# Attention kernel on one core: first queries in two loads, second key group and first values requested together, two more shared chunks, first output batch in two pieces

## The chip, the cores and the metric

The kernel runs on one core of a Trainium2 chip. The metric is the device time of one execution in microseconds (us). The kernel before took 522.69 us in the median of five runs (521.66 to 522.73). One more execution was recorded by the hardware profiler; it took 522.24 us, and its profile is the one read here.

## The reference: what is computed

Grouped-query attention with a softmax over 512 keys and no mask:

```python
B, Hq, Hkv, Sq, Sk, D = 16, 32, 8, 288, 512, 128      # bf16
k, v = repeat(k, 4, axis=1), repeat(v, 4, axis=1)
p = softmax(einsum("bhqd,bhkd->bhqk", q, k) * D ** -0.5)
out = einsum("bhqk,bhkd->bhqd", p, v)
```

Four query heads share one key/value head. So there are 16 x 8 = 128 groups, each with 4 x 288 = 1152 query rows, 512 keys and 512 value rows.

## The kernel before

**Tiling.** A group's 1152 query rows are nine tiles of 128 (t = 0 to 8), its 512 keys four tiles of 128 (j = 0 to 3). The scores are made transposed, keys on the partitions, so each pair (t, j) is a block of 128 columns: 36 blocks for a group. They are packed into three chunks of 1536 columns, which is three PSUM banks of 512 (`CH`, `BANK`, `TPC = 3`). Function `place` (L356) says where: chunk 0 holds t 0-3 with j 0, 1 and 2, one bank each; chunk 1 holds t 0-3 with j 3, then t 4-7 with j 0 and 1; chunk 2 holds t 4-7 with j 2 and 3, then t 8 with all four j. Over the 128 groups the chunks are numbered n = 0 to 383.

**One chunk.** TensorE makes the scores S(n) in one of two PSUM halves of `ps_s` (`op_s`, L420; the matmuls are on L439). ScalarE takes the exponential of the chunk from PSUM to `pt_sb` in bf16 (`op_exp`, L498; L516, or L511 for all but the last piece where a chunk is cut). TensorE multiplies the exponentials by the values: batch PV(r), r = 0 to 383, makes the three output tiles t = 3b to 3b + 2 (b = r mod 3) with twelve matmuls of 129 columns (`op_pv`, L462; L479); the 129th column is the sum of the row, since `v_sb` holds a column of ones. VectorE takes the reciprocal of the sums (`op_rc`, L573, L575) and multiplies (`op_ev`, L578, L585) into `o_sb`, which SyncE stores (`op_store`, L332).

**Shared chunks.** In every sixth chunk from n = 6 (`shared`, L519) the last 120 columns are kept from ScalarE. TensorE makes their scores by a matmul of its own in a corner of `ps_o` (`op_sy`, L445, L450; it waits until the output batch n - 3 has been evicted), and VectorE makes their exponential with a polynomial: `op_y`, `op_yb`, two in `op_ym`, `op_yu` three times, `op_yp` (L527 to L556), eight instructions spread over two rounds of its loop. There are 63 such chunks, n = 6 to 378.

**The order is written out by engine.** TensorE: warm-up matmuls; transposes of group 0's keys (`op_kt`, L399, L404); then for each n S(n), the shared piece if there is one, and PV(n - 2). At n = 2 the keys of group 1 are transposed between S(2) and PV(0) (L663, L664). VectorE first copies the transposed keys of groups 0 and 1 to `kt_sb` (`op_kc`, L408, L411): group 0 in two copies (key tile 0, then 1 to 3), group 1 in one. Then it goes through r: reciprocal, shared work, eviction. GpSimd copies the values of each group from `vd_sb` to `v_sb` (`op_vc`, L561, L568). PV of a group waits for that copy. S(n) waits for its queries (`have_q`), its keys (`have`) and for the exponential of chunk n - 2, which frees its PSUM half.

**The first chunks.** Chunks n < `FIRST` = 2 are cut into three exponentials of one bank each, as is the last one, 383. For these the matmuls of a bank signal it alone (`s_s0`), the exponentials signal each (`s_eb`), and consumers wait for the bank they need (`ready`, L374).

**The first loads.** SyncE's queue takes, in this order (L626, L627): the queries of group 0 as one transposing DMA of nine tiles (`op_q0`, L313, L316), the values of group 0 (128 KB, `op_v`, L302), the queries of group 1 (L311), the keys of groups 2 and 3 (transposing, L291), the values of groups 1 to 3 (384 KB), the queries of groups 2 and 3. ScalarE's queue takes the keys of group 0 (128 KB, not transposed, L676 and L283), then runs a small exponential, waits until VectorE has made both copies of group 0's keys (`s_k0` at 2, L678), issues the load of group 1's keys (128 KB, L680), and only then begins the exponentials. All later loads and stores are on SyncE's queue, ordered by due times in chunks (L630 to L642).

Of the kernel before, what the change touches and what calls it, by code (L numbers as in the profile page):

```python
# [131 lines left out]
def bass_standalone__gqa_softmax__near_ridge_kernel(  # L132
# [37 lines left out]
    NQ = 12  # L170
    NPT = 6
    WARM = 5
    FIRST = 2
    FIRST_SHARED = 6
    AHEAD = 1.08
    NO = 12
    NS = NG * NC
    LASTG = NG - 1
    ALONE = 8 * TPC


# [6 lines left out]
    with ExitStack() as es:  # L188
# [123 lines left out]

        def op_q0(i):  # L313

            c0, c1 = 0, NT
            nc.sync.dma_start_transpose(qt_sb[:, 0, c0:c1], q_v[0:P, c0 * D:c1 * D]).then_inc(sem["s_qp%d" % i], 16)  # L316

        def have_q(g, i):
            if g == 0:
                return ("s_qp0", 16)  # L320
            return ("s_q%d" % (g % NQ), 16 * (g // NQ + (0 if g % NQ == 0 else 1)))

        def have(kind, g):
# [46 lines left out]
        def used(i):  # L370

            return max(b for b in range(NC) for t in range(b * TPC, (b + 1) * TPC) for j in range(NJ) if place(t, j)[0] == i)

        def ready(n, x):  # L374

            if n < FIRST and x < TPC - 1:
                return ("s_eb", n * (TPC - 1) + x + 1)
            return ("s_e", n + 1 + (x if n == NS - 1 else 0))

        def sequence(b):  # L380

# [38 lines left out]
        def op_s(n):  # L420
            eng = nc.tensor
            g, i = n // NC, n % NC
            sl, gi = (g // UG) % NSLOT, g % UG
            waits = [have("k", g), have_q(g, i)]
            if n >= 2 + FIRST:
                waits.append(("s_e", n - 1))
            qg = qt_sb[:, g % NQ].rearrange("d t p -> d (t p)")
            todo = pieces(i)
            for x, (c, j, t, w) in enumerate(todo):
                if shared(n) and c + w == CH:  # L430
                    w -= W
                w_x = waits if x == 0 else []
                if n == 0 and x < 2:
                    w_x = [("s_k0", 1), waits[1]] if x == 0 else waits[:1]
                if n == 1 and x < 2:
                    w_x = [have_q(g, x)]
                if 2 <= n < 2 + FIRST:
                    w_x = w_x + [ready(n - 2, c // BANK)]
                ins = emit(eng, w_x, lambda: eng.matmul(  # L439
                    ps_s[:, n % 2, c:c + w], kt_sb[:, sl, j, gi, :], qg[:, t * P:t * P + w], start=True, stop=True))  # L440
                if n < FIRST and (c + w) % BANK == 0 and c + w < CH:
                    ins.then_inc(sem["s_s0"], 1)
            ins.then_inc(sem["s_s"], 1)

# [14 lines left out]
                return ps_s[:, 0, 0:TPC * DV].rearrange("p (a e) -> p a e", e=DV)  # L459
            return ps_o[:, r % 2, 0:TPC * DV].rearrange("p (a e) -> p a e", e=DV)  # L460

        def op_pv(r):  # L462
            eng = nc.tensor
            g = r // NC
            sl, gi = (g // UG) % NSLOT, g % UG
            waits = [("s_vc", g + 1)]
            if 2 <= r < NS - 2:
                waits.append(("s_ev", r - 1))
            if r == NS - 2:
                waits.append(("s_e", NS - 1))  # L470


            todo = sequence(r % NC)
            for x, (t, j) in enumerate(todo):
                i, c = place(t, j)
                w_x = (waits if x == 0 else []) + [ready(g * NC + i, c // BANK)]
                if c == CH - P and shared(g * NC + i):
                    w_x.append(("s_yp", nth(g * NC + i)))
                ins = emit(eng, w_x, lambda: eng.matmul(  # L479
                    outs(r)[:, t - r % NC * TPC, :], pt(g, t, j), v_sb[:, sl, gi * NJ + j, 0:DV], start=(x == 0),  # L480
                    stop=(t not in [y[0] for y in todo[x + 1:]]), skip_group_check=True))
            ins.then_inc(sem["s_pv"], 1)

        def op_pv_last():

# [12 lines left out]
        def op_exp(n):  # L498
# [6 lines left out]
            parts = [(0, CH)]  # L505
            if shared(n):
                parts = [(0, CH - W)]
            if n < FIRST or n == NS - 1:
                parts = [(x, x + BANK) for x in range(0, CH, BANK)]
            for x, (c, e) in enumerate(parts[:-1]):  # L510
                ins = emit(eng, [("s_s0", (TPC - 1) * n + x + 1)] if n < FIRST else waits, lambda: eng.activation(  # L511
                    d[:, c:e], s[:, c:e], ACTF.Exp, scale=scale))
                ins.then_inc(sem["s_e" if n == NS - 1 else "s_eb"], 1)
            parts = [(d[:, c:e], s[:, c:e]) for (c, e) in parts[-1:]]
# [2 lines left out]


        def shared(n):  # L519
            return FIRST_SHARED <= n < NS - NC and (n - FIRST_SHARED) % EVERY == 0  # L520

        def nth(n):
            return (n - FIRST_SHARED) // EVERY + 1

        def op_y(n):
            eng, b = nc.vector, nth(n) % NB
# [96 lines left out]
                op0=ALU.is_lt, op1=ALU.add)).then_inc(sem["s_bad"], 1)  # L623


        first = [lambda: op_q0(0), lambda: op_v(0, None, 0, 1)]  # L626
        first += [lambda: op_q(1), lambda: op_k(0, 2), lambda: op_v(0, None, 1, UG), lambda: op_q(2), lambda: op_q(3)]  # L627

        sp = []
# [23 lines left out]
        def _(eng):  # L653
# [5 lines left out]
            for n in range(NS):  # L659
# [2 lines left out]
                    op_sy(n)  # L662
                if n == 2:  # L663
                    op_kt(1, range(NJ), 1)  # L664
                if n >= LAG:
                    op_pv(n - LAG)
            op_pv(NS - 2)
            op_pv_last()
# [6 lines left out]
        def _(eng):  # L675
            op_kd(eng, 0)  # L676
            eng.activation(dum[:], nc.const_aps.tensor(0.0, [P, 1], FP32), ACTF.Exp)
            for (s, n) in need(eng, [("s_k0", 2)]):  # L678
                eng.wait_ge(s, n)
            op_kd(eng, 1)  # L680
            for n in range(NS):
                op_exp(n)
# [84 lines left out]
```

## Time and profile before

| What | Value |
|---|---|
| median of five runs | 522.69 us (521.66 to 522.73) |
| profiled execution | 522.24 us |
| its span, first to last instruction | 520.5 us |
| TensorE matmuls, busy | 509.7 us (98%), 6118 recorded |
| ScalarE, busy | 513.4 us (99%) |
| VectorE, busy | 369.1 us (71%) |
| GpSimd, busy | 79.6 us (15%) |
| granted TensorE clock | 1.00 |
| first exponential starts | 4.91 us |
| last exponential of the first three chunks ends | 9.30 us |
| next exponential (chunk 3) starts | 9.84 us |
| last exponential (chunk 383, third piece) starts | 516.37 us |

All positions are microseconds from the start of the span. An engine's busy time counts its instructions from start to end; matmuls and exponentials overlap their neighbours, so a busy engine need not be the one that sets the pace. A row of the timeline joins neighbouring instructions of the same kind: start, length from the first start to the last end, engine, line, what is written and read, how many; in brackets the idle time of that engine before it and what ended it. PE is TensorE's matmuls, PEld its weight loads, DVE VectorE, ACT ScalarE, POOL GpSimd, SP SyncE; a q behind the name means the DMA-issuing queue of that engine.

### The profile page before, as it was taken

The page shows a single profiled execution, that of the slowest core. Times are in us where ns is not written, and L with a number is a line of the kernel's source. Part 1 is how long each engine was busy: PE and PEld are TensorE (multiplying, and loading weights), DVE is VectorE, ACT ScalarE, POOL GpSimd, SP SyncE. Part 2 cuts the span into 40 slices and gives each one's busy share as a digit, 9 for nine tenths or more (in the row PEclk, how much of TensorE's full clock was granted, in tenths as well). Part 3 has the DMA queues.
Part 4 walks back from the last instruction along what each step waited for, and adds up shares of the span by engine and source line. Part 5 has one row for each costly group of instructions (what it writes and reads, how often), then busy time and mean ns, then how long its engine had stood idle before and what let it go on. Part 6 is the DMA issues. An engine that isn't in the chain of part 4 may idle for free.

```text
span 520.5 us, 15243 instructions
## 1 busy us (share of the span) xinstructions
PE 509.7 (98%) x6118; PEld 394.4 (76%) x6224; DVE 369.1 (71%) x1315; ACT 513.4 (99%) x393; POOL 79.6 (15%) x135
## 2 busy tenths in 40 slices
PE   8999999999999999999999999999999999999997
PEld 4777777777777777777777777777777777777776
DVE  2767777677677677676776776767767767677776
ACT  6999999999999999999999999999999999999997
POOL 2111111111111111111111111111111111111110
PEclk9999999999999999999999999999999999999999
DMA  9999999999999999999999999999999999998212
GB/s 183 239 212 255 247 190 228 241 210 220 193 259 252 196 259 202 234 225 210 248 247 210 215 229 226 237 185 199 251 215 237 219 194 217 196 241 185 90 69 93
DMA packets 253078, 110.06 MB, mean 211 GB/s; under 512 B 219728, under 2 KB 236752, under 8 KB 253008
## 3 DMA queue, kind: packets, MB, share of 16 engines
q1 hardware_dynamic: 252720, 108.82, 99.4%
q8 instruction: 49, 0.80, 0.7%
q10 hardware_dynamic: 288, 0.26, 0.2%
q14 instruction: 21, 0.17, 0.1%
HBM read 17.04 MB, written 37.75 MB: 105 GB/s over the span
## 4 chain that ended last, share of the span: by engine, by line
ACT 97%; PE 1%; DMA 1%; issue 1%; DVE 0%
ACT pt_sb L516 97%; DMA kd_sb<-in_k_dram 1%; PE ps_o L417 0%; ACT pt_sb L511 0%; PE ps_o L404 0%; PE ps_s L439 0%; PE ps_o L479 0%; DVE o_sb L585 0%; DVE o_sb L595 0%; PE ps_s L479 0%; DVE kt_sb L411 0%; DVE rl_sb L575 0%; PE ps_o L669 0%; DVE bad_sb L621 0%; DVE flag_i L734 0%
## 5 line engine op out<-in xcount | busy, mean ns | idle before, releaser
L516 ACT ACTIVATE pt_sb<-ps_s 128x1536 bf16<-128x1536 f32 (+2 forms) x384 | 509.0, 1441 | 0.5 <-PE ps_s L439 0.5
L479 PE MATMUL ps_o<-v_sb,pt_sb 128*128 128x129 bf16 x4584 | 322.1, 220 | 1.1
L479 PEld LDWEIGHTS ps_o<-v_sb,pt_sb 128*128 128x128 bf16 x4584 | 282.7, 98 | 49.6 <-DVE o_sb L585 13.8
L439 PE MATMUL ps_s<-qt_sb,kt_sb 128*128 128x512 bf16 (+2 forms) x1430 | 290.0, 320 | 5.1 <-DMA qt_sb<-in_q_dram 0.5
L585 DVE TENSOR_TENSOR o_sb<-ps_o,rl_sb 128x384 bf16<-128x384 f32 x382 | 211.7, 554 | 9.3 <-DVE rl_sb L575 0.5
L439 PEld LDWEIGHTS ps_s<-qt_sb,kt_sb 128*128 128x128 bf16 x1536 | 123.7, 98 | 62.1 <-DMA qt_sb<-in_q_dram 0.7
L575 DVE RECIPROCAL rl_sb<-ps_o 128x3 f32<-128x3 f32 x382 | 67.7, 177 | 125.8 <-PE ps_o L479 124.3
L568 POOL COPY v_sb<-vd_sb 128x512 bf16<-128x512 bf16 x128 | 78.6, 615 | 429.8 <-PE ps_o L479 412.9
L549 DVE SCALAR_TENSOR_TENSOR u_sb<-u_sb,m_sb 128x120 f32<-128x120 f32 x126 | 35.6, 282 | 2.2
L556 DVE SCALAR_TENSOR_TENSOR pt_sb<-u_sb,e_sb 128x120 bf16<-128x120 f32 x63 | 17.8, 283 | 2.2
L549 DVE SCALAR_TENSOR_TENSOR u_sb<-m_sb 128x120 f32<-128x120 f32 x63 | 17.4, 276 | 0.0
L527 DVE TENSOR_SCALAR y_sb<-ps_o 128x120 f32<-128x120 f32 x63 | 15.9, 252 | 0.0
L540 DVE TENSOR_SCALAR m_sb<-t_sb 128x120 int32<-128x120 int32 x63 | 14.0, 223 | 2.2
L450 PE MATMUL ps_o<-qt_sb,kt_sb 128*128 128x120 bf16 x63 | 13.6, 216 | 0.0
L540 DVE TENSOR_SCALAR e_sb<-t_sb 128x120 int32<-128x120 int32 x63 | 13.6, 215 | 0.0
L533 DVE TENSOR_SCALAR t_sb<-y_sb 128x120 int32<-128x120 f32 x63 | 13.4, 212 | 0.0
L450 PEld LDWEIGHTS ps_o<-qt_sb,kt_sb 128*128 128x128 bf16 x63 | 6.2, 98 | 7.4
L411 DVE COPY kt_sb<-ps_o 128x128 bf16<-128x128 bf16 (+2 forms) x3 | 1.0, 335 | 6.9 <-PE ps_o L404 6.8
L511 ACT ACTIVATE pt_sb<-ps_s 128x512 bf16<-128x512 f32 x6 | 3.3, 616 | 2.2 <-PE ps_s L439 2.2
L611 DVE TENSOR_REDUCE st_sb<-rl_sb 128x1 f32<-128x72 f32 (+1 forms) x16 | 3.5, 216 | 0.0
L613 DVE TENSOR_REDUCE st_sb<-rl_sb 128x1 f32<-128x72 f32 (+1 forms) x16 | 3.4, 215 | 0.0
L417 PE MATMUL ps_o<-const-bfloat16-1.0 128*128 128x512 bf16 (+1 forms) x6 | 2.4, 570 | 0.9 <-PEq L752 0.9
(32 smaller groups left out, 11.9 us busy)
## 6 DMA issues: line engine op xcount, KB each, us to landing
out_dram<-o_sb SPq DMA_DIRECT2D x127, 288.0 KB, 4.0
vd_sb<-in_v_dram SPq DMA_DIRECT2D x31, 512.0 KB, 5.6
qt_sb<-in_q_dram SPq DMA_TRANSPOSE x128, 5.2
kt_sb<-in_k_dram SPq DMA_TRANSPOSE x32, 5.3
vd_sb<-in_v_dram SPq DMA_DIRECT2D x1, 384.0 KB, 4.7
out_dram<-o_sb SPq DMA_DIRECT2D x3, 96.0 KB, 1.6
kd_sb<-in_k_dram ACTq DMA_DIRECT2D x2, 128.0 KB, 3.0
vd_sb<-in_v_dram SPq DMA_DIRECT2D x1, 128.0 KB, 3.5
```

Of the source, the lines that this page charges most:

```text
L439: ins = emit(eng, w_x, lambda: eng.matmul(ps_s[:, n % 2, c:c + w], kt_sb[:, sl, j, gi, :], qg[:, t * P:t * P + w], start=True, stop=True))
L450: emit(eng, [("s_ev", n - LAG - 1)], lambda: eng.matmul(ps_o[:, (n - LAG) % 2, BANK - W:BANK], kt_sb[:, (g // UG) % NSLOT, j, g % UG, :], ...
L479: ins = emit(eng, w_x, lambda: eng.matmul(outs(r)[:, t - r % NC * TPC, :], pt(g, t, j), v_sb[:, sl, gi * NJ + j, 0:DV], start=(x == 0), st ...
L516: emit(eng, waits, lambda: eng.activation(d, s, ACTF.Exp, scale=scale)).then_inc(sem["s_e"], 1)
L527: emit(eng, [("s_yb", nth(n) - NB), ("s_pv", n - LAG + 1)], lambda: eng.tensor_scalar(out=y_sb[:, b], in0=ps_o[:, (n - LAG) % 2, BANK - W: ...
L533: emit(eng, [("s_ym", 2 * (nth(n) - NB)), ("s_y", nth(n))], lambda: eng.tensor_scalar(out=t_sb[:, b], in0=y_sb[:, b], scalar1=Y_MUL, scala ...
L540: emit(eng, [("s_yp", nth(n) - NB), ("s_yb", nth(n))], lambda: eng.tensor_scalar(out=dst[:, b], in0=t_sb[:, b], scalar1=mask, scalar2=bits ...
L549: lambda: eng.scalar_tensor_tensor(out=u_sb[:, b, x], in0=src, scalar=QUARTIC[x], in1=m, op0=ALU.add, op1=ALU.mult)
L556: lambda: eng.scalar_tensor_tensor(out=pt_sb[:, n % NPT, CH - W:CH], in0=u_sb[:, b, 2], scalar=QUARTIC[3], in1=e_sb[:, b].bitcast(FP32), o ...
L568: emit(eng, waits, lambda: eng.tensor_copy(v_sb[:, sl, gi * NJ:(gi + 1) * NJ, 0:D], vd_sb[:, sl, gi].rearrange("p (j d) -> p j d", d=D))). ...
L575: emit(eng, [("s_pv", r + 1)], lambda: eng.reciprocal(rl_sb[:, TPC * r:TPC * (r + 1)].unsqueeze(2), outs(r)[:, :, D:DV])).then_inc(sem["s_ ...
L585: emit(eng, waits, lambda: eng.tensor_tensor(out=o_sb[:, g % NO, t0:t0 + TPC, :], in0=outs(r)[:, :, 0:D], in1=rl_sb[:, TPC * r:TPC * (r + ...
```

## The change

1. The queries of group 0 are loaded by two transposing DMAs, tiles 0 to 3 and tiles 4 to 8, each with a semaphore of its own. Chunk 0 waits for the first alone; chunk 1 waits for the second at its second matmul.
2. The load of group 0's values leaves SyncE's queue and goes to ScalarE's, in front of the load of group 1's keys. ScalarE issues both when the first copy of group 0's keys is made (`s_k0` at 1) and no longer waits for the second.
3. Chunks cut into pieces are given by a table, `PARTS`: chunk 0 in three banks as before, chunk 1 in two pieces (bank 0; banks 1 and 2), chunk 2 in two (banks 0 and 1; bank 2), chunk 383 in three. The waits by bank reach one chunk further (`FIRST = 3`).
4. Chunks 3 and 381 are shared too, so 65 chunks are, and the others keep their places.
5. PV(0) is issued in two pieces: the nine matmuls that read chunk 0 stay after S(2) and the transposes of group 1's keys; the three that read chunk 1 come after S(3) and its shared piece, before PV(1).

```diff
-    FIRST = 2
-    FIRST_SHARED = 6
+    FIRST = 3
+    PARTS = {0: (1, 2, 3), 1: (1, 3), 2: (2, 3), NG * NC - 1: (1, 2, 3)}
+    SHARED = [NC] + list(range(2 * NC, NS - NC, EVERY)) + [NS - NC]
...
         def op_q0(i):
-            c0, c1 = 0, NT
+            c0, c1 = ((0, TB), (TB, NT))[i]
...
             if g == 0:
-                return ("s_qp0", 16)
+                return ("s_qp%d" % min(i, 1), 16)
...
         def ready(n, x):
-            if n < FIRST and x < TPC - 1:
-                return ("s_eb", n * (TPC - 1) + x + 1)
-            return ("s_e", n + 1 + (x if n == NS - 1 else 0))
+            p = part(n, x)
+            if n < FIRST and p < len(PARTS[n]) - 1:
+                return ("s_eb", ahead(n) + p + 1)
+            return ("s_e", n + 1 + (p if n == NS - 1 else 0))
...
-        def op_pv(r):
+        def op_pv(r, some=slice(None)):
...
-            for x, (t, j) in enumerate(todo):
+            for x, (t, j) in list(enumerate(todo))[some]:
...
-            ins.then_inc(sem["s_pv"], 1)
+            if x == len(todo) - 1:
+                ins.then_inc(sem["s_pv"], 1)
...
-        first = [lambda: op_q0(0), lambda: op_v(0, None, 0, 1)]
+        first = [lambda i=i: op_q0(i) for i in range(2)]
...
                 if n == 2:
                     op_kt(1, range(NJ), 1)
-                if n >= LAG:
+                    op_pv(0, slice(0, TPC * TPC))
+                elif n == 3:
+                    op_pv(0, slice(TPC * TPC, None))
+                    op_pv(1)
+                elif n > 3:
                     op_pv(n - LAG)
...
-            for (s, n) in need(eng, [("s_k0", 2)]):
+            for (s, n) in need(eng, [("s_k0", 1)]):
                 eng.wait_ge(s, n)
+            op_v(0, eng, 0, 1)
             op_kd(eng, 1)
```

## The prediction on record

> **What bounds the kernel now.** I read the page's chain first. It gives ScalarE 97%; but the chain only says which engine's work follows on itself, and TensorE is 98% busy as well. So I looked at TensorE's timeline in the steady part.
>
> ```profile
> 16.97 0.81 PE L439 MATMUL ps_s<-qt_sb,kt_sb 128*128 128x512 bf16 x3
> 17.62 0.84 PE L479 MATMUL ps_o<-v_sb,pt_sb 128*128 128x129 bf16 x12
> 18.30 0.81 PE L439 MATMUL ps_s<-qt_sb,kt_sb 128*128 128x512 bf16 x3
> ```
>
> Each length reaches over the next start, so read the starts: three score matmuls take 0.65 us, twelve PV matmuls 0.68 us (0.0567 each), 1.33 a chunk, and no gap is left between them. The windows of one six-chunk period say the same: from 21.83 to 29.82 TensorE is busy 7.89 of 7.99 us. Now ScalarE, in the chain in order of time:
>
> ```profile
> 3.90 0.37 DVE kt_sb L411
> 4.27 0.02 issue
> 4.29 3.65 DMA kd_sb<-in_k_dram
> 7.94 0.05 issue
> 7.99 0.40 PE ps_o L404 x4
> 8.38 0.68 PE ps_o L479 x12
> 9.07 0.75 PE ps_s L439 x3
> 9.81 0.02 issue
> 9.84 3.96 ACT pt_sb L516 x3
> 13.80 0.05 issue
> 13.85 7.94 ACT pt_sb L516 x6
> 21.78 0.05 issue
> 21.83 7.93 ACT pt_sb L516 x6
> ```
>
> Chunks 3 to 5 are whole: 9.84 to 13.85, 1.34 each. The next six hold one shared chunk and take 21.83 - 13.85 = 7.98, 1.33 each. A share takes 120 of 1536 columns from ScalarE and the period does not get shorter. ScalarE is therefore fed by TensorE; both run at 1.33 us a chunk, and the gapless stream of matmuls from S(3) on sets the end. What counts is **when that stream starts and how much is in it**. It starts with S(3), behind the chain above: keys of group 1 asked for at 4.29, landed 7.94, transposed 7.99, copied by VectorE, S(3).
>
> ```profile
> 7.99 0.40 PE L404 MATMUL ps_o<-ident,kd_sb 128*128 128x128 bf16 x4 [1.05 <-DMA kd_sb<-in_k_dram]
> ...
> 8.22 0.84 PE L479 MATMUL ps_o<-v_sb,pt_sb 128*128 128x129 bf16 x12
> 8.42 0.42 DVE L411 COPY kt_sb<-ps_o 128x512 bf16<-128x512 bf16 x1 [4.17 <-PE ps_o L404]
> ...
> 8.99 0.81 PE L439 MATMUL ps_s<-qt_sb,kt_sb 128*128 128x512 bf16 x3
> ...
> 9.84 1.45 ACT L516 ACTIVATE pt_sb<-ps_s 128x1536 bf16<-128x1536 f32 x1 [0.54 <-PE ps_s L439]
> ```
>
> Call K the start of the transposes (7.99). PV(0) fills 8.22 to 8.90; VectorE's copy ends at 8.84 and lets S(3) go at 8.99 = K + 1.00. TensorE had idled 1.05 us before K, and ScalarE, cut for cut, could have started chunk 3 at 9.13 instead of 9.84: its pieces of one bank start 0.48 apart, the last of chunk 1 at 7.32, so chunk 2 at 7.80, and a whole chunk takes 1.33.
>
> **The change part by part.** The sum is made against the profiled execution: 522.24, of which the span is 520.50 and 1.74 lies around it. The median is 0.45 above it; the sum of the changes is carried over to the median.
>
> *Asking for K of group 1.* The first key copy starts at 3.58 and takes 0.22, so ends at 3.80; the second ends at 4.26 and the load was issued 0.03 later. Now ScalarE goes on at 3.83, issues V's load first (its two issues in the trace took 0.38 and 0.34) and K's at about 4.20: **0.09 earlier**. The new second Q load may hold back group 0's keys and eat this; bounds -0.15 to +0.25.
>
> *Its landing.* Before, 3.65 after the issue. The nearest rows: the same size with only the first Q load beside it landed after 2.4; V, behind Q in SyncE's queue, 3.5 (2.25 to its GpSimd copy at 5.76); three times the size, 4.7. V's 128 KB are now directly in front of K's in the same queue, but gone from SyncE's, whose load of Q of group 1 and keys of groups 2 and 3 lose V's 0.56 us of issue in front of them and gain one more Q issue (Q's nine tiles took 1.37 in one piece; two pieces cost between 0 and another 0.5). Bounds 2.4 and 4.7. I take 3.25, nearer to the old 3.65 because the same neighbours are on the engines, a little under it because they come earlier. So K = 4.20 + 3.25 + 0.05 = 7.50: **-0.49** (ends: 6.65, -1.34, and 8.95, +0.96).
>
> *V.* It now arrives much later than 5.71, but PV(0) needs it only after the transposes. GpSimd's copy takes 0.61. If V lands 0.4 before K the copy ends at 7.05 + 0.05 + 0.61 = 7.71, PV(0) is free to start at K + 0.23 = 7.73: nothing. If it lands with K, PV(0) starts at 8.16, its nine matmuls end at 8.67, and S(3), queued behind them, is 0.17 late. I take 0, since V is first in the queue.
>
> *PV(0) in two pieces.* S(3) waits for VectorE's copy at K + 1.00, and even all twelve matmuls are through at K + 0.91. Moving three of them behind S(3) therefore does not bring S(3) forward; it adds them to the gapless stream: 3 x 0.0567 = **+0.17**. It would be free only if V were the late one.
>
> *Q in two loads, earlier first exponential.* The first exponential can start when ScalarE has issued its two loads, about 4.20 + 0.35 + 0.03 = 4.58 instead of 4.91. This 0.33 ends in TensorE's wait before K, which takes 1.05: **0**. It counts only if K comes before 6.65 or so. Chunks 1 and 2 are cut into two and two pieces where it was three and one; four either way, so ScalarE's sum stays (three pieces take 6.36 - 4.91 = 1.45 against 1.33 whole, so a cut costs about 0.06).
>
> *Chunk 3 shared.* TensorE's block is 0.003 longer (392 and 120 columns run 0.166 + 0.053 for 0.216). ScalarE is 0.10 shorter there (a whole chunk's 1.33 less a bank's 0.48 is 0.83 ns a column over 1024 columns, times 120), while S(4), a whole PV(1) and three matmuls away, is what chunk 4 waits for: **0**. VectorE gets its eight operations among evictions that TensorE needs. At chunk 6 the reciprocal before them starts at 14.51 and the second eviction after it ends at 16.91 + 0.55 = 17.46, 2.95 later. Here that reciprocal follows PV(1), at K + 1.00 + 0.65 + 0.17 + 0.68 + 0.25 = K + 2.75, so batch 2 is evicted by K + 5.70. PV(4), which needs that bank, starts at K + 5.81: S(4) at K + 2.50, PV(2) 0.65 later, and two rounds of 1.33. It just fits; 0 to +0.1.
>
> *Chunk 381 shared.* The exponential of 383 began at 515.42, 0.06 after the last S(383) matmul, and cannot move before it: gain 0 to -0.02. The shared matmul must wait for the eviction of batch 377, which the shared work of chunk 378 and the reductions of L725 hold until 512.46, and would stand at 511.89 + 0.60 = 512.49: a wait up to 0.05. VectorE then catches up before the reciprocal at 517.02 (its idle there is 0.17 and 0.56 before the one of 516.08). **+0.02**, ends -0.02 and +0.3 if VectorE's backlog reaches the last reciprocal.
>
> Sum: -0.49 + 0.17 + 0.02 = **-0.30**; profiled time 521.94, median 522.39, about 522.4.
>
> **Two rules.** The six-chunk period shows that a share returns nothing. The Trainium skill, page "ScalarE: Activation LUTs", section "What ACT_TABLE_LOAD costs", gives 0.833 ns per element, so by estimate 120 columns are worth 0.10, two more shares -0.20, and the sum would be -0.50 if ScalarE set the pace. The trace's period speaks against it: ScalarE isn't the pacer.
>
> The first 128 KB load landed after 2.4 and the second, with two transposing loads beside it, after 3.65. The page "DMA: Bandwidth & Descriptors", section "Issuing engines are not separate DMA queues", says that a second issuing engine saves issue time only, since all share the 16 engines; by it V's move would leave K landing no sooner than before, 7.85 to 7.95, and the sum, by estimate, would be near +0.1. That rule speaks against part 2 of the change.
>
> **Rivals.** *A: K lands as before or a little later*, 7.90 to 8.30 (3.65 to 4.1 after the issue). For it: the same neighbours, V in front. Then -0.09 to +0.31, plus 0.19: +0.1 to +0.5, about 523.0 in the middle. *B: the queue clears and K lands as the first load did*, at 6.60. For it: 2.4 was measured; against it: only one transposing load ran beside that one. Then -1.34 + 0.17 = -1.17, 521.5. ScalarE's own pace allows no more: from 4.58 three, two and two pieces (4.20) bring chunk 3 to 8.78 and chunk 4, after a shared 1.23, to 10.01 against 11.19. *C, slower: V is the late one.* Two loads side by side land like the 384 KB, 4.7 after V's issue at 3.83, at 8.53; copy, wakes and nine matmuls add 0.05 + 0.61 + 0.05 + 0.51: S(3) at 9.73, and with 0.17 and 0.02 the end is +0.93 (+1.2 if two tenths more). It decides from V landing at 7.6 on, where S(3) in effect is where it was. *D: the split changes no wait at all*, because K still waits for what held it to 7.94: +0.1, within A.
>
> **How the numbers follow.** Forecast (K 7.1 to 7.9, -0.7 to +0.1): 0.60. A: 0.20. B: 0.12. C: 0.08. About 0.2% or 1.05 us is what a measurement of this kernel can tell from no change; the five runs spread as much. Only B's far end (beyond -1.05) and C's far end are outside. B and some low outliers give 0.11 faster, C 0.06 slower, the rest is the same. The range takes in the forecast, A up to its end (+0.5, 523.2) and most of B (-1.17, 521.5, and 0.1 for the runs' scatter): 521.4 to 523.2. C is left out.
>
> **What would show it.** Right: first exponential at about 4.6, transposes of group 1 at about 7.5, S(3) 1.0 after, PV(0)'s last three behind S(3), chunk 4 about 3.37 after K (before 3.20), then 1.33 a chunk with 7.98 for six. Wrong: transposes after 8.0 (A), before 6.9 (B), a GpSimd copy of V that ends after K + 0.3 with TensorE idle behind it (C), a period other than 7.98, or idle time of TensorE in the last 10 us.

## The result, and the profile after

The changed kernel takes **523.09 us** in the median of 28 runs (522.59 to 525.11), the kernel before, run beside it, 522.45 us in the median of 48 (521.66 to 523.29). The ratio is 1.0016 (95% interval 1.0011 to 1.0021): 0.64 us slower by the medians, 0.84 (0.57 to 1.10) by the ratio, where 0.30 less was forecast. The time lies in the range (521.4 to 523.2); the sign is wrong.

The profiled execution of the changed kernel took 525.49 us, 2.4 above its median, and TensorE ran 3.41 us of it at half clock; of 30 executions three show this (a mean granted clock of 0.997, the others 0.999 or 1.000), so a second profile of the same kernel (523.05 us, granted clock 1.00, called the repeat below) is the one that the terms are compared with.

First the chain of waits of the first profile, in order of time (start, length, what). It answers to the chain shown of before.

```profile
3.40 0.23 DVE kt_sb L421
3.64 0.02 issue
3.66 0.35 ACTq L303
4.01 0.03 issue
4.04 5.33 DMA kd_sb<-in_k_dram
9.38 0.05 issue
9.42 0.40 PE ps_o L414 x4
9.82 0.51 PE ps_o L489 x9
10.33 0.05 issue
10.38 1.09 PE ps_s L449 x3
```

The keys of group 1 are asked for 0.25 earlier than before (4.04, not 4.29), behind 0.35 of V's issue, and land 5.33 later instead of 3.65. The steady part is as it was. The repeat's timeline of TensorE, the rows that answer to the three of before:

```profile
17.55 0.81 PE L449 MATMUL ps_s<-qt_sb,kt_sb 128*128 128x512 bf16 x3
18.20 0.84 PE L489 MATMUL ps_o<-v_sb,pt_sb 128*128 128x129 bf16 x12
18.88 0.81 PE L449 MATMUL ps_s<-qt_sb,kt_sb 128*128 128x512 bf16 x3
```

The starts are 0.65 and 0.68 apart again, 1.33 a chunk. From chunk 20 to chunk 379 every kernel of this study takes 477.60 us. From there to chunk 383 they differ by 0.06 at most. The rest of the differences lies in front of chunk 20, behind chunk 383 and outside the span. So the two profiles can be laid side by side by stretches:

| Stretch (us) | before | first profile | repeat | forecast of the difference | repeat less before |
|---|---|---|---|---|---|
| start of span to K, the transposes of group 1's keys | 7.99 | 9.42 | 8.02 | -0.49 | +0.03 |
| K to the exponential of chunk 4 | 3.20 | 4.96 | 3.30 | +0.17 | +0.10 |
| chunk 4 to chunk 20 | 21.28 | 21.31 | 21.73 | 0 to +0.1 | **+0.45** |
| chunk 20 to chunk 383 | 482.95 | 482.99 | 482.99 | +0.02 | +0.04 |
| chunk 383 to the end of the span | 5.08 | 4.96 | 4.96 | 0 | -0.12 |
| around the span | 1.74 | 1.85 | 2.05 | 0 | +0.31 |
| sum | 522.24 | 525.49 | 523.05 | -0.30 | +0.81 |

Three rows are off: K did not come earlier, something between chunk 4 and chunk 20 takes 0.45, and 0.31 more lies outside the span. The repeat's chain of waits shows the second:

```profile
9.97 0.02 issue
10.00 0.19 DVE rl_sb L586
10.19 0.02 issue
10.21 0.56 DVE o_sb L596
10.77 0.09 DVE rl_sb L586
10.86 0.17 DVE y_sb L538
11.03 0.47 DVE o_sb L596
11.49 0.60 DVE t_sb L544
...
13.33 0.28 DVE pt_sb L567
13.62 0.48 DVE o_sb L596
14.10 0.05 issue
14.14 0.23 PE ps_o L460
```

For four microseconds the chain runs through VectorE, not through TensorE. It ends in L460, the shared matmul of chunk 6, which waits until three batches, 0 to 2, have been evicted (the words "output batch n - 3" in the description above count them from one). Two rows of the repeat's timeline, of GpSimd and of VectorE, show why that eviction is late:

```profile
10.83 1.17 POOL L579 COPY v_sb<-vd_sb 128x512 bf16<-128x512 bf16 x2 [3.95 <-DMA vd_sb<-in_v_dram]
11.41 0.68 DVE L544 TENSOR_SCALAR t_sb<-y_sb 128x120 int32<-128x120 f32 x1
```

L544 takes 0.22 in its mean over the kernel. Here it runs beside GpSimd's copies of the values of groups 1 and 2, takes 0.68 and ends 0.08 after the second copy. What TensorE loses by it shows in the score matmuls and the shared matmul of chunk 6, before (first two rows) and in the repeat:

```profile
12.98 0.76 PE L439 MATMUL ps_s<-qt_sb,kt_sb 128*128 128x512 bf16 x3
13.58 0.22 PE L450 MATMUL ps_o<-qt_sb,kt_sb 128*128 128x120 bf16 x1
13.14 0.76 PE L449 MATMUL ps_s<-qt_sb,kt_sb 128*128 128x512 bf16 x3
14.14 0.23 PE L460 MATMUL ps_o<-qt_sb,kt_sb 128*128 128x120 bf16 x1 [0.24 <-DVE o_sb L596]
```

Without a wait the shared matmul starts 0.60 after the start of its chunk's score matmuls, here 1.00: 0.40 lost.

The third row shows on no engine. In each of the ten profiles of this study with both new shares, the trace's DMA records hold one more packet of instructions, 8 KB, that starts 1.80 to 1.86 after the end of the span; the ten others have none. The time around the span is 1.84 to 2.13 in the former, in each of them 0.32 less than where this packet ends, and 1.69 to 1.74 in the latter. So the two shares, 20 instructions more for VectorE, go with another 0.1 to 0.4 there (0.24 by the means). That it is their own instructions that are loaded fits, but no run shows it.

### The profile page after: what moved, and what is told of

The parts are those of the page before. It is cut to its first block, busy times and chain, and to the rows that moved or that the text cites. A ratio compares the mean times of both kernels' runs of the same rounds, so it can differ in the third digit from the quotient of the medians.

```text
span 523.6 us, 15268 instructions
## 1 busy us (share of the span) xinstructions
PE 511.2 (98%) x6120; PEld 395.4 (76%) x6226; DVE 371.6 (71%) x1331; ACT 513.5 (98%) x393; POOL 79.4 (15%) x135
## 4 chain that ended last, share of the span: by engine, by line
PE 96%; issue 1%; DMA 1%; DVE 1%; ACTq 0%
PE ps_o L489 50%; PE ps_s L449 45%; DMA kd_sb<-in_k_dram 1%; PE ps_o L460 1%; PE ps_o L427 0%; DVE o_sb L596 0%; DVE u_sb L560 0%; DVE rl_sb L586 0%; PE ps_o L414 0%; DVE o_sb L606 0%; ACTq L303 0%; DVE pt_sb L567 0%; DVE kt_sb L421 0%; DVE m_sb L551 0%; PE ps_o L684 0%
## 5 line engine op out<-in xcount | busy, mean ns | idle before, releaser
L560 DVE SCALAR_TENSOR_TENSOR u_sb<-u_sb,m_sb 128x120 f32<-128x120 f32 x130 | 36.7, 282 | 2.3
L560 DVE SCALAR_TENSOR_TENSOR u_sb<-m_sb 128x120 f32<-128x120 f32 x65 | 17.9, 276 | 0.0
L538 DVE TENSOR_SCALAR y_sb<-ps_o 128x120 f32<-128x120 f32 x65 | 16.4, 252 | 0.0
L551 DVE TENSOR_SCALAR m_sb<-t_sb 128x120 int32<-128x120 int32 x65 | 14.5, 223 | 2.2
L460 PE MATMUL ps_o<-qt_sb,kt_sb 128*128 128x120 bf16 x65 | 14.2, 218 | 0.0
L551 DVE TENSOR_SCALAR e_sb<-t_sb 128x120 int32<-128x120 int32 x65 | 14.0, 216 | 0.0
L544 DVE TENSOR_SCALAR t_sb<-y_sb 128x120 int32<-128x120 f32 x65 | 13.7, 211 | 0.0
L460 PEld LDWEIGHTS ps_o<-qt_sb,kt_sb 128*128 128x128 bf16 x65 | 6.4, 99 | 8.0 <-DVE o_sb L596 0.3
L522 ACT ACTIVATE pt_sb<-ps_s 128x512 bf16<-128x512 f32 (+1 forms) x6 | 3.9, 679 | 1.8 <-PE ps_s L449 1.8
```

The lines of the kernel that those rows point to most:

```text
L460: emit(eng, [("s_ev", n - LAG - 1)], lambda: eng.matmul(ps_o[:, (n - LAG) % 2, BANK - W:BANK], kt_sb[:, (g // UG) % NSLOT, j, g % UG, :], ...
L538: emit(eng, [("s_yb", nth(n) - NB), ("s_pv", n - LAG + 1)], lambda: eng.tensor_scalar(out=y_sb[:, b], in0=ps_o[:, (n - LAG) % 2, BANK - W: ...
L544: emit(eng, [("s_ym", 2 * (nth(n) - NB)), ("s_y", nth(n))], lambda: eng.tensor_scalar(out=t_sb[:, b], in0=y_sb[:, b], scalar1=Y_MUL, scala ...
L551: emit(eng, [("s_yp", nth(n) - NB), ("s_yb", nth(n))], lambda: eng.tensor_scalar(out=dst[:, b], in0=t_sb[:, b], scalar1=mask, scalar2=bits ...
L560: lambda: eng.scalar_tensor_tensor(out=u_sb[:, b, x], in0=src, scalar=QUARTIC[x], in1=m, op0=ALU.add, op1=ALU.mult)
```

## The experiments

Each kernel is named by its label; "before" is the kernel before, run on the same chip in the same session. K is the start of the transposes of group 1's keys in the kernel's profile.

**The same kernel again** (`a0_after_again`, no edit).

> The changed kernel once more, unchanged, because its profiled execution (525.49) lies 2.4 above its median (523.09) and shows a granted clock of 0.55 from 10.4 to 14.2. Theories A (the second Q load takes a whole issue of 1.26 us on SyncE's queue, so the Q load of group 1 and the keys of groups 2 and 3 meet V and K of group 1), B (V in front of K in ScalarE's queue delays K) and C (what was added to the stream of matmuls, three PV matmuls and two shares, and not the arrival of K) all expect +0.64 in the median. A and B expect the transposes of group 1 at about 8.4 to 8.6 in an execution without the low clock (median loss 0.64 less 0.19 for the stream, after 7.99); C expects them at 8.0 to 8.1.

522.91 against 521.93 us: 1.0020 (1.0011 to 1.0028). Its profile is the repeat shown above.

### Is it the share of chunk 3?

**Chunk 3 not shared** (`c1_no_share_3`).

```diff
-    SHARED = [NC] + list(range(2 * NC, NS - NC, EVERY)) + [NS - NC]
+    SHARED = list(range(2 * NC, NS - NC, EVERY)) + [NS - NC]
```

> The changed kernel without the share in chunk 3 (that of 381 stays). New theory E, from the second profile of the changed kernel: K of group 1 lands there when it did before (8.0), and the loss is that the shared matmul of chunk 6 waits 0.52 for the eviction of batch 2, which VectorE's work for chunk 3 holds back. E: 0.5 less than the changed kernel, so +0.1 to +0.4 against before (0.17 for the three PV matmuls, 0.04 for the share of 381). If instead the late K (theories A, B) made the loss: no difference to the changed kernel, +0.6 to +0.9.

522.46 against 522.01: 1.0006 (0.9997 to 1.0015). The gap at chunk 6 is gone. Against the changed kernel's 1.0020 and 1.0016 that is 0.5 to 0.7 us, though the intervals touch. The packet of instructions behind the span is gone as well (1.74 around it), so not all of this is the gap. GpSimd's copies run here too (10.40 to 11.57), beside reciprocals and evictions only; those keep their 0.17 and 0.56.

**The share kept, one of GpSimd's copies moved** (`c3_v_copy_later`): the copy of group 2's values waits for two batches more.

```diff
-                waits.append(("s_pv", NC * (g - 2) + 2))
+                waits.append(("s_pv", NC * (g - 2) + (4 if g == 2 else 2)))
```

> The changed kernel, with GpSimd's copy of the values of group 2 held until batch 3 is made (it waits for batch 1 in the changed kernel). Theory F, a part of E: VectorE's shared work of chunk 3 is late because its operations from SBUF to SBUF stand still beside GpSimd's copies (L544 took 0.68 instead of 0.21 beside the copies of 10.83 to 12.00). F: L544 takes 0.2 to 0.3, TensorE's wait before the shared matmul of chunk 6 falls from 0.52 to 0.1 or less, time 0.4 to 0.5 less than the changed kernel. Rival: VectorE is late because it simply has too much in these rounds; then L544 is short but the wait stays at 0.3 or more, or the eviction is late all the same, and the time is as with the changed kernel.

522.52: 1.0008 (0.9999 to 1.0017). VectorE's timeline, the operation that stood still before and the eviction that the shared matmul waits for:

```profile
11.28 0.38 DVE L544 TENSOR_SCALAR t_sb<-y_sb 128x120 int32<-128x120 f32 x1
...
13.10 0.55 DVE L596 TENSOR_TENSOR o_sb<-ps_o,rl_sb 128x384 bf16<-128x384 f32 x1
```

The first copy (10.96 to 11.57) still holds L544 for a moment; the second no longer does. In front of the shared matmul the matmuls' starts are 0.27 apart where 0.17 is usual: 0.10 is left of the 0.40. Nothing of the share was changed; so it is not the share's work that stalls TensorE here, but its standing beside the copies. The trace shows this; the median alone would not, since its interval overlaps those of the changed kernel.

**The two shares alone** on the kernel before (`b2_shares`).

```diff
-            return FIRST_SHARED <= n < NS - NC and (n - FIRST_SHARED) % EVERY == 0
+            return n in SHARED
```

> The kernel before with the two shares alone. E: the shared matmul of chunk 6 waits as in the changed kernel (0.3 to 0.6), +0.04 for 381: +0.3 to +0.6 against before. If shares cost nothing by themselves (as predicted): 0.0 to +0.1.

522.58 against 522.01: 1.0011 (1.0002 to 1.0020), 0.57 slower with none of the other parts. Its VectorE rows:

```profile
11.09 0.51 DVE L540 TENSOR_SCALAR m_sb<-t_sb 128x120 int32<-128x120 int32 x1
11.52 0.64 DVE L540 TENSOR_SCALAR e_sb<-t_sb 128x120 int32<-128x120 int32 x1
```

The copies ran from 10.88 to 12.08. With K at 7.38 another operation is hit, L540, and twice. The starts in front of the shared matmul are 0.82 apart.

Whether the copies hit the share depends on when K comes. In five profiles with the share and a later K (the first profile, `a1_q_one_load`, `a3_pv_whole`, `a4_k_first` and `g1_fill_wait`, K from 8.48 to 9.42) L544 starts 0.07 to 0.09 after the end of the second copy and takes 0.21, and the shared matmul of chunk 6 doesn't wait. In `h2_sync_plus_one`, with K at 8.05 and the copies 0.28 earlier than in the repeat, L544 takes 0.35 and the shared matmul is 0.08 late. So a late K and this stall rather replace each other than add up.

### Is it the loads?

**One load of the queries** (`a1_q_one_load`).

```diff
-            c0, c1 = ((0, TB), (TB, NT))[i]
+            c0, c1 = 0, NT
...
-        first = [lambda i=i: op_q0(i) for i in range(2)]
+        first = [lambda: op_q0(0)]
```

> The changed kernel with the queries of group 0 in one load again. A: SyncE issues the Q load of group 1 at 2.25 instead of 3.50 and it lands before 6.5; K of group 1 lands at 7.4 to 7.6, the transposes start at about 7.5, time against before -0.3 (-0.49 for K, +0.19 for the stream). B: K still lands at 8.4 or later, +0.5 to +0.7. C: K's arrival doesn't matter, +0.6.

524.11: 1.0052 (1.0038 to 1.0066), 1.2 slower than the changed kernel. The idea that the second issue holds the keys back fell: the nine tiles land at 4.99 where the first four land at 3.58 in the repeat, the first exponential starts at 5.68 instead of 4.52, and K is 9.04. Behind the longer wait for them a score matmul took 0.43 until 8.0, and 0.22 from then on.

**The values back on SyncE's queue** (`a2_v_on_sync`), behind both query loads.

```diff
-        first = [lambda i=i: op_q0(i) for i in range(2)]
+        first = [lambda i=i: op_q0(i) for i in range(2)] + [lambda: op_v(0, None, 0, 1)]
...
-            op_v(0, eng, 0, 1)
```

> The changed kernel with the values of group 0 back on SyncE's queue, behind the two Q loads; ScalarE asks for K of group 1 alone at 3.7. B: K lands 3.65 after that as before, transposes at 7.4, time against before -0.4 (-0.59 + 0.19). A: the Q load of group 1 is issued at 4.1, later still, and K meets it: transposes at 8.2 or later, +0.4 or more. C: +0.6.

523.01: 1.0021 (1.0012 to 1.0030). K's load lands 2.54 after its issue, at 6.20, and K is 6.32: with V on the other queue the key load is 1.4 faster. The loads behind V on SyncE's queue come 0.6 later, too (the queries of group 1 are issued at 4.13, not 3.51), which may be a part of it. But the time doesn't move. PV(0) has to wait for V's copy until 7.30, and chunk 3's shared work is hit twice by the copies of groups 1 and 2. A part of the chain of waits:

```profile
6.63 0.62 POOL v_sb L579
7.26 0.05 issue
7.30 0.68 PE ps_o L489 x9
...
10.73 0.22 DVE m_sb L551
10.95 0.55 DVE e_sb L551
11.50 0.62 DVE u_sb L560
```

The shared matmul of chunk 6 comes 0.75 late (starts 0.92 apart). What K gained by coming 1.7 earlier than in the repeat is spent: 0.77 between K and chunk 4, 0.38 more than the repeat loses at chunk 6, and 0.58 behind chunk 383 (the late last store, at the end of this document).

**PV(0) whole, in its old place** (`a3_pv_whole`).

```diff
-                    op_pv(0, slice(0, TPC * TPC))
-                elif n == 3:
-                    op_pv(0, slice(TPC * TPC, None))
-                    op_pv(1)
-                elif n > 3:
+                if n >= LAG:
                     op_pv(n - LAG)
```

> The changed kernel with PV(0) in one piece again, before S(3). A and B: S(3) starts at the transposes plus 1.00, as with the split, and the stream behind it is 3 x 0.0567 = 0.17 shorter: 0.17 less than the changed kernel, so +0.47 against before. C, if it is the split that costs: +0.1 or less against before. If the split hides a late V (copy of GpSimd ending later than the transposes start): no difference or slower than the changed kernel.

522.83: 1.0016 (1.0008 to 1.0025), not to be told from the changed kernel's 522.91. From K to chunk 4 it takes 3.18 against 3.30.

**Keys ahead of values** on ScalarE's queue (`a4_k_first`): the two lines exchanged.

> The changed kernel with K of group 1 asked for ahead of V on ScalarE's queue. B (V in front costs K about 1.5: 2.5 after its issue without V in front, 3.8 to 4.2 with it): K lands at 6.2 to 6.8, V now at 7.5 to 8, so GpSimd's copy ends at 8.2 to 8.6 and S(3), behind nine PV matmuls, starts at 8.8 to 9.2 as in the changed kernel: no difference to it, +0.6 to +0.9 against before. If V's place is nothing to K: K lands near 8, transposes at 8, the same time too; the two differ in where TensorE waits, for GpSimd's copy (B) or for the load of K.

524.58: 1.0046 (1.0029 to 1.0064), in two groups of three runs, 523.5 to 523.7 and 525.5 to 525.8. In its profile, which is of the lower group, group 0's keys came late (3.81), a score matmul took 0.43 and the full clock was granted from 9.99 on, the key load landed 3.47 after its issue, V 0.50 later, and V's copy ended at 9.08, 0.60 after K.

**Loads and cuts alone** (`e1_loads_only`): neither chunk 3 nor 381 shared, PV(0) whole.

```diff
-    SHARED = [NC] + list(range(2 * NC, NS - NC, EVERY)) + [NS - NC]
+    SHARED = list(range(2 * NC, NS - NC, EVERY))
```

> The changed kernel without both new shares and with PV(0) whole: what is left is the loads and the cuts of chunks 1 and 2. E (the share of chunk 3 costs about 0.5, the split 0.17, the share of 381 0.04, the loads nothing): 0.0 to +0.2 against before, K of group 1 landing at 7.9 to 8.4. If the loads cost by themselves: +0.4 or more. If they gain what was predicted (K at 7.5): -0.4.

522.50 against 522.16: 1.0009 (1.0000 to 1.0018). K is 8.33; no gain is left of the loads even without the shares.

**Both asked for at once, at the start** (`d1_loads_at_once`), on `e1_loads_only`.

```diff
             op_kd(eng, 0)
+            op_kd(eng, 1)
+            op_v(0, eng, 0, 1)
```

> The changed kernel without both new shares, with PV(0) whole, and with K and V of the first groups asked for at the very start on ScalarE's queue, in the order K of group 0, K of group 1, V, ahead of its wait. The theory that the arrival of K sets the start of the stream: transposes of group 1 at 6.4 to 6.8, right behind S(2); ScalarE then sets the pace up to chunk 4, which starts at 9.9 to 10.2 instead of 11.19, time -0.9 to -1.2 against before. Rival: the first Q and K loads are slowed by the two more loads beside them, the first exponential moves from 4.5 to 5 or later, and what is left is -0.5 or less.

523.00 against 522.01: 1.0015 (1.0006 to 1.0025). The keys land at 4.64 and the values at 5.08, and both then wait. The price is paid by the first queries: they land at 4.85 instead of about 3.6, the score matmuls behind them take 0.43 each until 8.3, K is 8.71 and chunk 4 at 12.04.

**The values between the two query loads** (`d2_v_between_q`), on `e1_loads_only`, V on SyncE's queue.

```diff
-        first = [lambda i=i: op_q0(i) for i in range(2)]
+        first = [lambda: op_q0(0), lambda: op_v(0, None, 0, 1), lambda: op_q0(1)]
```

> No new shares, PV(0) whole, V on SyncE's queue between the two Q loads, K of group 1 alone on ScalarE's queue when the first copy is made. E and B together: V landed by 5.5, K by 6.4, transposes at 6.4 to 6.6, chunk 4 starts at 10.1 to 10.4 (before 11.19), nothing given back at chunk 6: -0.7 to -1.0 against before. Rival: the second Q load, now issued at 2.8, lands after 6 and chunk 1 waits for it, or the loads of group 1 meet K: chunk 4 at 10.9 or later, -0.3 or less.

523.48 against 522.16: 1.0026 (1.0014 to 1.0037), in two groups (522.4 to 523.1 and 523.9 to 524.7). The keys land at 6.71, but chunk 1 waits for the second query load:

```profile
6.98 1.26 PE L449 MATMUL ps_s<-qt_sb,kt_sb 128*128 128x512 bf16 x8 [1.36 <-DMA qt_sb<-in_q_dram]
```

**The same with PV(0) whole behind S(3)** (`d3_pv0_after_s3`).

> As the kernel with V between the Q loads, but with all of PV(0) after S(3), so that S(3) waits for the keys alone and not for V. If V is late there (copy of GpSimd ending after the transposes): 0.1 to 0.4 faster than that kernel. If V is in time: the twelve matmuls that filled the wait for VectorE's copy (0.68 of it) go into the stream, up to 0.4 slower, unless ScalarE is still the one that sets the pace there; then no difference.

524.37: 1.0042 (1.0026 to 1.0057). S(3) starts 0.95 after K and all twelve matmuls follow it; chunk 4 is at 12.07.

### What is an earlier start worth?

**Values behind the queries on SyncE, no new shares, PV(0) whole** (`f1_v_behind_q`; `a2_v_on_sync` with the two edits of `e1_loads_only`).

> V on SyncE's queue behind both Q loads, K of group 1 alone on ScalarE's queue, no new shares, PV(0) whole. Its twin with shares and split landed K at 6.2 and started chunk 4 at 10.40 (before 11.19), and gave it all back waiting 0.86 for VectorE before chunk 6's shared matmul. If the arrival of K sets the time once that wait is gone: chunk 4 at 10.1 to 10.5, -0.7 to -1.0 against before. If the arrival of K does not matter, or that execution was a lucky one: within 0.3 of before.

522.20 against 521.78: 1.0007 (0.9998 to 1.0016). K is 6.89 and chunk 4 starts at 10.22, 0.97 earlier than in the profile of before. Then PV(3) stands still until GpSimd has copied group 1's values, which landed at 10.88:

```profile
10.68 0.82 PE L449 MATMUL ps_s<-qt_sb,kt_sb 128*128 128x512 bf16 x6
11.69 0.84 PE L489 MATMUL ps_o<-v_sb,pt_sb 128*128 128x129 bf16 x12 [0.19 <-DVE o_sb L596]
```

The bracket names an eviction that ended at 11.66; but that is batch 2's, and PV(3) needs batch 1's, which was through long before. The copy, 10.93 to 11.55, is what PV(3) needs. 0.35 is lost here, 0.45 more at the end (below).

**The key load alone asked for earlier** (`f4_k_only`), on the kernel before.

```diff
-            for (s, n) in need(eng, [("s_k0", 2)]):
+            for (s, n) in need(eng, [("s_k0", 1)]):
```

> The kernel before with one number changed: ScalarE asks for K of group 1 when the first key copy is made, not the second (about 0.45 earlier), V and Q as before. If an earlier request brings K earlier: transposes at 7.0 to 7.6 instead of 8.0, -0.3 to -0.6. If K is held by the loads of SyncE's queue and not by its own request: 0.0, between -0.1 and +0.1.

521.70 against 521.78: 1.0000 (0.9991 to 1.0008). K is 7.55 in its profile, 0.44 before the one of before; the median doesn't know of it. The profile of before, 522.24, lies above the medians of before on the later chips (521.78 to 522.16): its K of 7.99 was probably a late one; in the profile of `b2_shares`, whose loads are those of before, it is 7.38.

**One wait more on SyncE** (`h2_sync_plus_one`), a redundant one, after its first loads.

```diff
+            eng.wait_ge(sem["s_qp0"], 16)
```

> The changed kernel with one redundant wait more on SyncE, behind the first loads, where its semaphore has long been reached. In all four kernels that had V on SyncE's queue and Q in two loads (one instruction more on SyncE than the kernel before) the last store was issued 0.35 after its release instead of 0.05 and the flag load took 0.72 instead of 0.47; in the other eleven never. If it is the number of SyncE's instructions: the same 0.35 and 0.72 here, +0.4 against the changed kernel. If it is V's load on that queue: 0.05 and 0.47, no difference.

522.81 against 521.85: 1.0014 (1.0005 to 1.0023), as the changed kernel; last store 0.03 after its release. An instruction more on SyncE does not make the store late.

**One store less** (`h1_one_store_less`), on `f1_v_behind_q`: the first two output batches of the last group are stored together.

> The kernel with V behind both Q loads (f1: +0.42 against before, although chunk 20 starts 0.6 earlier than in the profile of before), with the first two of the last three stores made one, so that SyncE has two instructions less. If the number of SyncE's instructions makes the late last store: 0.05 and 0.47 again, 0.4 to 0.5 less than f1, 0.0 against before. If not: +0.4 as f1.

521.68 against 521.85: **0.9991 (0.9982 to 1.0000)**. This is the lowest of the study, and at the edge of what can be told from before. The tail is as short as it was, and K is 6.55.

**The values of groups 1 to 3 sooner** (`h3_values_sooner`), on `h1_one_store_less`.

```diff
+        op_v(0, None, 1, UG)
         op_k(0, 2)
```

> As the kernel with one store less, and the values of groups 1 to 3 asked for ahead of the keys of groups 2 and 3. In f1 PV(3) waited 0.35 for GpSimd's copy of group 1's values, which landed at 10.88. If that is what is late next: they land at 9 to 9.6, no wait of TensorE between chunk 4 and the end, -0.3 to -0.4 against the kernel with one store less, and -0.3 against before, or -0.3 less than f1 if the tail stays. If the keys of groups 2 and 3 become late (S(6) waits for them): no gain.

521.95: 0.9998 (0.9989 to 1.0007). The values land at 9.47, PV(3) no longer waits, chunk 7 starts at 14.34 against 14.61, and the profiled execution, 521.38, is the shortest of all profiles. Its median is not.

**The wait for the queries filled with matmuls** (`g1_fill_wait`), on `a1_q_one_load`: three warm-up matmuls of 512 columns in place of one of 128.

> The changed kernel with the queries in one load, and three 512-column warm-up matmuls instead of one of 128 in TensorE's wait for them. The theory that the kernel with one Q load lost so much (+2.2, runs from 523.4 to 526.1) because TensorE's wait of 1.4 before S(0) lets the clock fall to half for the next stretches (its records grant full clock only from 8.0 on): the granted clock is full by 4.6 to 5.5, median at most 523.3, spread under 1.2. If it lost because its first exponential starts at 5.7 and K lands at 9.0: no difference, 523.5 or more.

523.65 against 521.78: 1.0033 (1.0021 to 1.0045). The score matmuls run at full speed from 6.55 instead of 8.03, and the runs spread 1.2 us instead of 2.7. Of the loss of `a1_q_one_load` (2.2 by the medians, 2.7 by the ratios) this takes back 0.3 or 1.0; the two intervals overlap. The larger part stays: the late queries (first exponential still at 5.73, K 8.94).

## Why the prediction was wrong

The reading of the bound held: the matmul stream is gapless at 1.33 a chunk, and shares return nothing in the steady part. So did the frame, K plus what is in the stream. Three terms of the sum failed. Between the forecast of -0.30 and the +0.81 of the two profiles lie 1.11: +0.52 for K, +0.45 for the stretch with the shared work of chunk 3, +0.31 outside the span, and -0.17 for the rest. The medians lie 0.94 from the forecast. Other executions divide the loss otherwise: K alone is 7.38 and 7.99 in the two profiles with the loads of before, and 7.89 to 9.42 in seven with those of the changed kernel.

**The step that failed in kind: "*Chunk 3 shared.* ... It just fits; 0 to +0.1".** It took 2.95 us, from the reciprocal to the second eviction, over from chunk 6, and put batch 2's eviction at K + 5.70, just ahead of what waits for it. The place was right: the reciprocal came at K + 2.67 (K + 2.75 in the prediction) and the waiting matmul was ready at K + 5.72. The duration was not: 3.39 in the repeat, 0.44 more, of which L544 alone has 0.46. The profile of before already showed what stands beside the two places, here its GpSimd copies from chunk 3 to chunk 6 and the operation that L544 was there:

```profile
10.54 1.17 POOL L568 COPY v_sb<-vd_sb 128x512 bf16<-128x512 bf16 x2 [4.17 <-DMA vd_sb<-in_v_dram]
...
14.54 0.61 POOL L568 COPY v_sb<-vd_sb 128x512 bf16<-128x512 bf16 x1 [2.83 <-PE ps_o L479]
...
15.24 0.21 DVE L533 TENSOR_SCALAR t_sb<-y_sb 128x120 int32<-128x120 f32 x1
```

At chunk 6 one copy runs and ends 0.09 before L533 starts. At chunk 3 the values of groups 1 and 2 are copied back to back, until 11.71. I priced VectorE's operations at a place where the copy just clears them and moved them to one where it doesn't. I also named PV(4) as the waiter; the shared matmul of chunk 6 stands just before it and waits for the same three evictions. `c1_no_share_3` and `c3_v_copy_later` each take the loss away, by different means, and `b2_shares` makes it alone; that the copies make this stall is shown. How much of the median it makes is less sure, since with a later K it is absent.

**The term that was mis-sized: K's landing.** I took 3.25 after the issue, between bounds of 2.4 and 4.7, and less than the old 3.65 because the neighbours would come earlier. They came later: the second query load cost SyncE's queue a whole issue of 1.26, where I had allowed 0 to 0.5, and V's 0.56 less didn't make up for it. The queries of group 1 were issued at 3.51 instead of 2.87, the keys of groups 2 and 3 at 4.90 instead of 4.23. The repeat has 3.95, `c1_no_share_3` 4.10, `c3_v_copy_later` 3.80, the first profile 5.33, outside my bounds. Without V in front, on the same queue, it was 2.54 (`a2_v_on_sync`), 3.09 (`f1_v_behind_q`), 2.74 (`h1_one_store_less`) and 2.84 (`h3_values_sooner`). So V's place on ScalarE's queue instead of SyncE's costs about a microsecond, and K is where it was (8.02). How much of that is V directly in front stays open: in these four the loads behind V on SyncE's queue came 0.6 later as well, and with V directly behind the keys instead (`a4_k_first`) the landing took 3.47, between the two. Rival A, to which I gave 0.20, is what happened: +0.1 to +0.5 by its terms, +0.03 + 0.10 + 0.04 = +0.17 in the repeat without the share.

The rule that I quoted against this part, that issuing engines share the same DMA engines (the Trainium skill, page "DMA: Bandwidth & Descriptors", section "Issuing engines are not separate DMA queues"), would have put the landing at 7.85 to 7.95; the repeat has 7.97. Yet with V behind the queries on SyncE's queue the keys landed at 6.20 to 6.84, so which queue takes a load did matter here.

**The term put at nothing: the time around the span.** The prediction took its 1.74 over unchanged and gave no reason. The repeat has 2.05, with the packet of instructions described above.

The other steps:

- *Asking earlier, 0.09*: right in kind. 4.02 in the repeat, 0.27 earlier, since group 0's keys came 0.2 sooner.
- *V at nothing*: right. Its copy ended at 6.88, before K. Rival C, the late V, did not happen; its sum gives 9.75, not 9.73. In the same way 4.1 after the issue is 8.35 in rival A, not 8.30.
- *PV(0) in two pieces, +0.17*: 0.10 to 0.12 from K to chunk 4 (3.30 against 3.20 and 3.18); nothing that a median resolves.
- *Earlier first exponential hidden*: right. It came at 4.52 (4.58 forecast); TensorE's wait in front of K grew from 1.05 to 1.47.
- *Chunk 381, +0.02*: +0.04, right; the shared matmul waited as said, and VectorE caught up.
- *Rival B*, the early K, became real in `a2_v_on_sync` and `f1_v_behind_q`, and brought none of the -1.17 it was priced at. I had let the start alone decide. The earlier start ran into what did not come earlier with it: the copy of V or of group 1's values, and in `a2_v_on_sync` chunk 3's shared work beside the copies; the late last store took the rest.

## What to carry to other kernels

Price a moved operation at its new place: look which other engine works on the same memory there, and if the trace shows no such pair, keep the range wide instead of copying a duration. Before putting a load on another engine's queue, ask what now stands behind it there, and what comes earlier in the old one; here nothing did, since a second query load took its place. When the start of a stream comes forward, follow the stream to the next arrival that does not.

## What the runs showed of the hardware that I had not expected

- **VectorE beside GpSimd.** VectorE's operations from SBUF to SBUF stood still while GpSimd copied from SBUF to SBUF: 0.68 (L544, the repeat), 0.51 and 0.64 (L540, `b2_shares`), 0.63 and 0.70 (L551 and L560, `a2_v_on_sync`) instead of 0.21 to 0.28, each ending 0.07 to 0.13 after a copy's end. Those that read PSUM kept their times (L538 0.25, evictions 0.55). The Trainium skill, page "SBUF — State Buffer", section "SBUF: two separate sides", says that the two engines share a pair of ports which one instruction holds as a whole while the other is blocked; ends tied to the copies' ends agree with that. It limits this to VectorE instructions in a mode that uses two ports or with two inputs from SBUF. L560 has two inputs; L544, L540 and L551 have one, and no run here shows in which mode they ran.
- **Half clock after a wait.** In the first profile TensorE waited 2.74 us for the keys. The granted clock then fell to half at 10.68, for 3.41 us; the windows of that profile (span, length, PE, PEld, DVE, ACT, POOL busy with counts, granted clock, DMA share, GB/s) show it:

```profile
8.00:10.38 2.38, 0.91 (x13) 0.76 (x14) 0.42 (x1) 0.93 (x2) 0.00 (x0) 1.00 1.22 240
10.38:14.20 3.82, 3.59 (x22) 2.53 (x24) 1.68 (x6) 1.35 (x1) 1.23 (x2) 0.55 1.19 240
14.20:18.40 4.20, 4.15 (x53) 3.30 (x53) 3.24 (x13) 4.01 (x4) 0.61 (x1) 1.00 1.06 205
```

  TensorE is busy 3.59 of 3.82 us and gets through 22 recorded matmuls where a like stretch later holds 53 in 4.20. A wait of 1.47 (the repeat) had no such effect. The length alone doesn't decide: behind waits of 1.08 and 0.97 for the first queries (`a1_q_one_load`, `d1_loads_at_once`) the score matmuls ran at half speed. In the first profile late keys thus cost twice. The two groups of runs, 1.6 to 2.0 us apart, in `a4_k_first`, `d2_v_between_q` and `d3_pv0_after_s3` are for the most part the same thing. The mean granted clock is 0.996 or 0.997, as in the first profile, in all three upper runs of the first, four of six of the second and two of three of the third, and 0.999 or 1.000 in every lower run.
- **A late last store.** Four kernels with one DMA more on SyncE's queue than before (`a2_v_on_sync`, `d2_v_between_q`, `d3_pv0_after_s3`, `f1_v_behind_q`) issue their last store 0.33 or 0.34 after the end of the last eviction, which releases it, instead of 0.03 or 0.04, and the tail behind chunk 383 takes 5.54 to 5.84 instead of 4.96 to 5.10. One store less (`h1_one_store_less`) puts it back to 0.03; a wait more (`h2_sync_plus_one`) doesn't bring it. It goes with the number of DMAs on the queue; the cause isn't shown. In these four a packet of 8 KB of instructions starts 1.00 to 1.02 after the release of that store, in the others 1.35 or more after it; whether loading instructions has to do with it, no run separates.
- **A transposing load's issue hardly depends on its size**: 1.21 to 1.32 us for four or five tiles, 1.37 or 1.38 for nine as the first load. Two loads for one therefore cost a whole issue more on the queue, and yet the changed kernel without the split (`a1_q_one_load`) was 1.2 us slower.

Open as well: why the earlier end of `h3_values_sooner` in its profile is not in its median.
